# Grouped-query attention with a cached K and V, on one core: all eight heads of the first projection per chunk, and its loads reordered over two DMA queues

## Chip, cores, metric

One core of a Trainium2 chip. The metric is device time in microseconds (us) of one execution, which most executions of a kernel here repeat within 0.3%. The profile's span is some 1.8 us shorter than the time.

## The reference

Two independent problems A and B of the same shape, bfloat16, whose outputs are concatenated:

```python
B, Sq, D = 16, 32, 1024            # 512 tokens
Hq, Hkv, Sk, Dh = 32, 4, 512, 128
q = (x @ wq).reshape(B, Sq, Hq, Dh).transpose(0, 2, 1, 3)
k, v = repeat(k_cache, 8, axis=1), repeat(v_cache, 8, axis=1)
p = softmax(einsum("bhqd,bhkd->bhqk", q, k) * Dh ** -0.5)
o = einsum("bhqk,bhkd->bhqd", p, v)
return o.transpose(0, 2, 1, 3).reshape(B, Sq, Hq * Dh) @ wo
```

## The kernel before

TensorE runs one long fixed sequence: queries, scores, values and output projections are interleaved so that it never has to wait. Only the first twenty microseconds have nothing to interleave: there the queries of the first eight heads (A's first key/value group) are made while their data arrive. The contraction over D = 1024 has eight chunks of 128. Chunks 0 and 1 of x are transposed on TensorE, the others by transposing DMA loads, two chunks each. Each head needs one matmul per chunk, 128x128 weights against 512 tokens.

```python
NF = REP - 2            # 6 heads at first: 8 - 2
HC = DC // 2            # 4 chunks per weight tile
...
load_x(TT // 2, TT, nc.scalar)                 # ScalarE's queue
nc.scalar.preload_act_table_set("natural_log_exp_and_others")
load_x(0, TT // 2)                             # SyncE's queue, as all without nc.scalar
load_w0(0, 1, 0, NF // 2)                      # load_w0(chunk from, to, head from, to)
load_w0(0, 1, NF // 2, NF)
load_w0(1, 2, 0, NF, nc.scalar)
load_x_transposed(2)                           # chunks 2 and 3 of x
load_w0(2, 3, 0, NF, nc.scalar)
load_w0(3, 4, 0, NF)
load_w0(0, HC, NF, REP)                        # heads 6 and 7, chunks 0 to 3
load_w0(HC, HC + 1, 0, REP)
load_x_transposed(HC)
...
warm_up(22)                                    # matmuls on constants
... # transposes of chunks 0 and 1
for ts in ((0, TT // 2), (TT // 2, TT)):
    first_heads(range(0, NF // 2), (0,), *ts)  # six half-width matmuls
first_heads(range(NF // 2, NF), (0,))
first_heads(range(NF), (1, 2, 3))
first_q += [...]                               # two more PSUM banks come free
first_heads(range(NF, REP), range(HC))
first_heads(range(REP), range(HC, DC - 1))
```

All loads are given to two queues, and the framework that builds the program (below: the builder) gives each DMA a semaphore, a counter that tells of its landing and for which an instruction can wait.

## Time and profile before

| kernel before | |
|---|---|
| time, median of 6 runs | 343.27 us (342.94 to 343.48) |
| span of the profiled run | 340.8 us |
| TensorE busy | 99% of the span |
| first projection, L531 | 67 matmuls, with starts from 4.2 to 18.2 us |

In the profile PE is TensorE's matmuls, PEld its weight loads, SPq and ACTq the queues on which SyncE and ScalarE issue DMAs; a line "start, length, what" in the chain of work tells what the end of the program waited for at that time. "q_ps L531" is the first projection, L301 the later ones. The prediction below shows and reads the lines.

### The profile page before, as it was taken

Reading aid. Unit: us, or ns where it says so; the run is one execution under the profiler, and the core shown is the slowest. Engines: PE = TensorE matmul, PEld = TensorE weight load, DVE = VectorE, ACT = ScalarE, POOL = GpSimd, SP = SyncE. Lnnn points to the kernel's source line nnn. Section 1 sums busy time; section 2 is a strip of 40 time slices with the busy share of each in tenths; the row PEclk is TensorE's granted clock in tenths of the full one; section 3 lists DMA queues with packets and bytes.
Section 4 is the critical chain, followed back from the end, with each engine's and each line's share of the span. In section 5 each row is a group of like instructions: output and inputs, shape, how many; then the busy total and the mean of one; then the engine's idle time right before and its main releaser. Section 6 shows DMA issues by size and latency. Waiting matters only on the chain.

```text
span 340.8 us, 5475 instructions
## 1 busy us (share of the span) xinstructions
PE 336.7 (99%) x2113; PEld 213.0 (62%) x2113; DVE 265.2 (78%) x335; ACT 185.4 (54%) x208; POOL 46.7 (14%) x206
## 2 busy tenths in 40 slices
PE   8999999999999999999999999999999999999996
PEld 5456666666666666666666666666666666666555
DVE  0047988888888898888888898879888888889540
ACT  2067666666757667666645544554554555555110
POOL 0001111011111111110012221222122101111100
PEclk9999999999999999999999999999999999999999
DMA  8999999989996998899999966998449996430001
GB/s 208 297 186 270 287 248 223 188 238 259 312 266 159 241 230 227 214 291 296 317 297 285 239 125 148 344 283 211 125 106 300 355 193 161 105 100 13 17 19 33
DMA packets 128622, 71.70 MB, mean 210 GB/s; under 512 B 76880, under 2 KB 127824, under 8 KB 128592
## 3 DMA queue, kind: packets, MB, share of 16 engines
q1 hardware_dynamic: 127504, 69.68, 84.1%
q0 software_dynamic: 384, 1.05, 0.9%
q10 hardware_dynamic: 704, 0.59, 0.6%
q8 instruction: 17, 0.28, 0.4%
q14 instruction: 13, 0.11, 0.1%
HBM read 50.59 MB, written 2.10 MB: 155 GB/s over the span
## 4 chain that ended last, share of the span: by engine, by line
PE 99%; ACT 0%; issue 0%; ACTq 0%
PE f_ps L320 32%; PE q_ps L301 28%; PE s_ps L357 16%; PE ob L425 16%; PE q_ps L531 4%; PE q_ps L513 1%; PE xT_ps L521 0%; ACT o_sb L329 0%; ACTq L329 0%
## 5 line engine op out<-in xcount | busy, mean ns | idle before, releaser
L365 ACT ACTIVATE p_sb<-s_ps,shift 128x1024 bf16<-128x1024 f32 x128 | 142.7, 1115 | 97.5 <-PE s_ps L357 85.0
L376 DVE TRANSPOSE_TENSOR_REDUCE parts<-p_sb 128x32 f32<-128x1024 bf16 x128 | 158.8, 1240 | 20.9 <-ACT p_sb L365 19.3
L320 PE MATMUL f_ps<-wo_sb,oT 128*128 128x512 bf16 (+1 forms) x544 | 132.3, 366 | 0.0
L301 PE MATMUL q_ps<-xT,wq_sb 128*128 128x512 bf16 x448 | 116.9, 379 | 0.0
L357 PE MATMUL s_ps<-qT,kT 128*128 128x256 bf16 x512 | 76.8, 273 | 0.0
L425 PE MATMUL ob<-p_sb,v_sb 128*128 128x256 bf16 x512 | 76.8, 273 | 0.0
L320 PEld LDWEIGHTS <-oT 128*128 128x128 bf16 x544 | 53.2, 98 | 35.3
L357 PEld LDWEIGHTS <-kT 128*128 128x128 bf16 x512 | 56.9, 113 | 28.3
L301 PEld LDWEIGHTS <-wq_sb 128*128 128x128 bf16 x448 | 43.8, 98 | 32.2
L425 PEld LDWEIGHTS <-v_sb 128*128 128x128 bf16 x512 | 50.1, 98 | 20.0
L447 DVE TENSOR_TENSOR oT<-r,ob 128x512 bf16<-128x512 f32 x64 | 43.9, 686 | 19.9 <-PE ob L425 19.4
L411 DVE STREAM_TRANSPOSE r<-rall 128x512 f32<-128x512 f32 x64 | 44.2, 691 | 1.1
L309 ACT CAST qT<-q_ps 128x512 bf16<-128x512 f32 x56 | 32.7, 583 | 16.5 <-PE q_ps L301 16.5
L394 POOL COPY half<-cs 64x32 f32<-64x32 f32 x32 | 6.5, 204 | 231.4 <-DVE cs L384 231.3
L329 ACT CAST o_sb<-f_ps 128x512 bf16<-128x512 f32 (+1 forms) x17 | 9.5, 559 | 23.6 <-PE f_ps L320 23.6
L531 PE MATMUL q_ps<-xT,w_sb 128*128 128x512 bf16 (+1 forms) x67 | 14.4, 374 | 0.0
L384 DVE TENSOR_REDUCE cs<-parts 128x32 f32<-128x128 f32 x32 | 12.0, 376 | 1.1
L406 DVE RECIPROCAL rall<-sums 128x32 f32<-128x32 f32 x32 | 10.2, 320 | 3.3 <-POOL sums L403 3.3
L553 DVE CAST qT<-q_ps 128x512 bf16<-128x512 f32 x4 | 2.5, 684 | 12.8 <-PE q_ps L531 12.8
L531 PEld LDWEIGHTS <-w_sb 128*128 128x128 bf16 x67 | 6.5, 100 | 7.5 <-DMA w_sb<-in_A_wq_dram 0.3
L553 ACT CAST qT<-q_ps 128x512 bf16<-128x512 f32 x4 | 2.1, 599 | 12.3 <-PE q_ps L531 12.3
L331 POOL DMA_DIRECT2D out_dram<-o_sb x8 | 4.6, 574 | 29.3 <-ACT o_sb L329 29.3
(25 smaller groups left out, 48.2 us busy)
## 6 DMA issues: line engine op xcount, KB each, us to landing
v_sb<-in_A_v_cache_dram SPq DMA_DIRECT2D x16, 512.0 KB, 6.0
wq_sb<-in_B_wq_dram SPq DMA_DIRECT2D x8, 1024.0 KB, 5.8
wo_sb<-in_A_wo_dram SPq DMA_DIRECT2D x8, 1024.0 KB, 7.6
v_sb<-in_B_v_cache_dram SPq DMA_DIRECT2D x16, 512.0 KB, 4.8
wo_sb<-in_B_wo_dram SPq DMA_DIRECT2D x8, 1024.0 KB, 8.5
wq_sb<-in_A_wq_dram SPq DMA_DIRECT2D x5, 1024.0 KB, 6.7
wq_sb<-in_A_wq_dram SPq DMA_DIRECT2D x2, 512.0 KB, 7.3
kT<-in_A_k_cache_dram SPq DMA_TRANSPOSE x64, 4.4
```

Of the source, the lines that this page charges most:

```text
L301: nc.tensor.matmul(ps[:], lhsT=w[:, dc, (h % 4) * DH:(h % 4 + 1) * DH], rhs=xT[pr][:, dc, :], start=(dc == 0), stop=(dc == DC - 1),)
L309: nc.scalar.copy(out=qT[pr, g][:, :, hl, :], in_=ps[:].rearrange("p (b s) -> p b s", s=SQ),)
L320: nc.tensor.matmul(ps[:, 0:width], lhsT=oT[pr, tt][:, h, :], rhs=wo_tiles[pr, nh, h // REP][:, h % REP, off:off + width], start=(h == 0), ...
L357: nc.tensor.matmul(s_ps[:, c, :], lhsT=kT[:, i % GRP, c, :], rhs=qT[pr, g][:, b, :, :].rearrange("p h s -> p (h s)"), start=True, stop=True,)
L365: nc.scalar.activation(out=p_sb[:], in_=s_ps[:], func=ACTF.Exp, bias=shift[:], scale=SCALE)
L376: nc.vector.tensor_reduce(out=parts[k][:, q, :, :].rearrange("p c h -> p (c h)"), in_=st[i]["p"][:].rearrange("p c (h s) -> p (c h) s", s=SQ),
L384: nc.vector.tensor_reduce(out=cs[:], in_=parts.pop(k)[:].rearrange("p q c h -> p q h c"), axis=AX.X, op=ALU.add,)
L406: nc.vector.reciprocal(out=rall[:, k, :], in_=quad.pop(k)[:])
L411: nc.vector.transpose(out=r[:].rearrange("p n s -> p (n s)"), in_=rall[:, k, o * 2 * REP:(o + 1) * 2 * REP] .unsqueeze(2).to_broadcast([P, ...
L425: nc.tensor.matmul(ob[j][:, q, :], lhsT=v_sb[:, i % GRP, c, :], rhs=st[i]["p"][:, c, :], start=(c == 0), stop=(c == KC - 1),)
L447: nc.vector.tensor_tensor(out=out, in0=rcp.pop(j)[:].rearrange("p (q h) s -> p q h s", h=REP), in1=ob.pop(j)[:].rearrange("p q (h s) -> p ...
L531: nc.tensor.matmul(first_q[h][:, ts], lhsT=w0[dc // HC][:, dc % HC, h * DH:(h + 1) * DH], rhs=xT[0][:, dc, ts], start=(dc == 0 and t0 == 0 ...
```

## The change

The intent: since the two banks of PSUM (the memory that TensorE's results go to) for heads 6 and 7 are free after chunk 1, all eight heads can be done from chunk 2 on (and heads 6 and 7 catch up on chunks 0 and 1), and the loads can then come in the order of need, spread over both queues.

```diff
             load_w0(0, 1, 0, NF // 2)
-            load_w0(0, 1, NF // 2, NF)
-            load_w0(1, 2, 0, NF, nc.scalar)
+            load_w0(0, 1, NF // 2, NF, nc.scalar)
+            load_w0(1, 2, 0, NF)
+            load_w0(0, 2, NF, REP, nc.scalar)
+            load_w0(2, 3, 0, REP, nc.scalar)
             load_x_transposed(2)
-            load_w0(2, 3, 0, NF, nc.scalar)
-            load_w0(3, 4, 0, NF)
-            load_w0(0, HC, NF, REP)
+            load_w0(3, HC, 0, REP)
@@
-            first_heads(range(NF), (1, 2, 3))
+            first_heads(range(NF), (1,))
             first_q += [psum.tile([P, NW], FP32, name="q_ps", tag="ob")[:] for _ in range(2)]
-            first_heads(range(NF, REP), range(HC))
-            first_heads(range(REP), range(HC, DC - 1))
+            first_heads(range(NF, REP), (0, 1))
+            first_heads(range(REP), range(2, DC - 1))
```

## The prediction

> **What bounds the kernel now.** I read the page first (busy shares and slices), then the chain of work that ended last in order of time, then the busy time by stretches, then the timeline of TensorE over the first 20 us, and last the DMA issues of that stretch. The question is only whether TensorE ever stands still, because every matmul of this program stays where the change leaves it.
>
> The page and the busy time by stretches:
>
> ```profile
> span 340.8 us, 5475 instructions
> PE 336.7 (99%) x2113; PEld 213.0 (62%) x2113; DVE 265.2 (78%) x335; ACT 185.4 (54%) x208; POOL 46.7 (14%) x206
> ...
> PE   8999999999999999999999999999999999999996
> ```
>
> ```profile
> 18.50:120.00 101.50, 101.50 (x632) 63.80 (x631) 83.90 (x104) 68.56 (x83) 12.95 (x60) 1.00 1.07 242
> 120.00:240.00 120.00, 120.00 (x764) 77.03 (x762) 104.55 (x131) 70.97 (x77) 20.28 (x84) 1.00 0.97 252
> ```
>
> The columns of the second fence are the stretch, its length, then PE, PEld, DVE, ACT and POOL busy. On the page all slices but the first and the last are at 90% or more; in the stretches PE is busy for 101.50 of 101.50 us and 120.00 of 120.00 us. A loaded engine can hide short gaps under pipelined matmuls, so I check the pace as well, in the chain:
>
> ```profile
> 0.93 2.52 PE q_ps L513 x22
> 3.45 0.95 PE xT_ps L521 x8
> 4.40 0.84 PE q_ps L531 x6
> 5.24 0.01 issue
> 5.25 13.36 PE q_ps L531 x61
> 18.61 3.45 PE q_ps L301 x16
> ```
>
> In the steady stream 16 matmuls of 512 columns take 3.45 us, 0.2156 us each. The 61 of the first projection take 13.36 us, 0.2190 each, so their surplus is 13.36 - 61 x 0.2156 = 0.21 us. That, plus whatever the first 6 lost, is the whole stock that a better start can draw on. The chain never leaves TensorE before its last half microsecond.
>
> Where the surplus lies is in the timeline of the start, cut into narrow windows so that a first start can be read off each line:
>
> ```profile
> 4.20 0.76 PEld L531 LDWEIGHTS <-w_sb 128*128 128x128 bf16 x6
> 5.24 2.08 PEld L531 LDWEIGHTS <-w_sb 128*128 128x128 bf16 x11 [0.29 <-DMA w_sb<-in_A_wq_dram]
> ```
>
> ```profile
> 4.75 0.89 PE L531 MATMUL q_ps<-xT,w_sb 128*128 128x256 bf16 x4
> ```
>
> ```profile
> 6.99 0.62 PE L531 MATMUL q_ps<-xT,w_sb 128*128 128x512 bf16 x2
> ```
>
> The six half-width matmuls start at 4.20; the fourth of them at 4.75, so three took 0.55 us, 0.18 each. The other three run at 0.11 each and are issued by 4.75 + 3 x 0.11 = 5.08. The next starts at 5.24 to 5.25, held by the weights of heads 3 to 5: a wait of **0.17 us** (the 0.29 is the weight-load side of the same wait). The last line holds the final matmul of chunk 1 (start 6.99) and the first of chunk 2; the second ends at 7.61 with a duration of 0.38, so it starts at 7.23, 0.24 after its predecessor in place of 0.216: a wait of **0.03 us**, on the arrival of chunk 2's transposed x. From there to 18.61 the pace is 0.2158.
>
> **What the Trainium skill says.** "TensorE: Matmul & The Clock Gate", part 1 on the clock gate: the array runs at half speed until it has been active for some 3.4 us of a free-running window, 106.7 ns against 55.6 ns for 128 columns, 426.7 against 215.7 ns for 512. The trace agrees: 22 warm-up matmuls of 128 columns need 2.52 us (0.107 apart plus the last one's tail), the full-width ones are 0.216 apart, and the step lies at about 4.7 us, between the third and fourth half-width matmul. The slow half-width matmuls are thus a matter of the clock, not of loads, and the change cannot buy back their 0.2 us. "DMA: Bandwidth & Descriptors", section "Issuing engines are not separate DMA queues": DMAs issued by different engines run on the same 16 DMA engines, and using several saves only issue time. Its section "Queues, rings and completion order": each DMA engine alternates between the queues that have work, packet by packet. So what moves to ScalarE's queue is not carried faster; it shares the bandwidth with SyncE's and passes what waits behind on that queue. The case's trace shows an issue costing 0.43 to 0.58 us for a plain load and 1.33 us for the first transposing one. The last column of these two stretches is the rate in GB/s, 354 and then 165 where the transposing load (256-byte packets) runs:
>
> ```profile
> 3.00:4.00 1.00, 1.00 (x12) 0.75 (x10) 0.20 (x1) 0.00 (x0) 0.00 (x0) 1.00 1.07 354
> 5.00:6.00 1.00, 0.99 (x7) 0.40 (x5) 0.00 (x0) 0.00 (x0) 0.00 (x0) 1.00 1.21 165
> ```
>
> The issues and landings:
>
> ```profile
> 1.25 0.93 SPq L474 DMA_DIRECT2D w_sb<-in_A_wq_dram  x2
> 2.22 1.33 SPq L468 DMA_TRANSPOSE xT<-in_A_x_dram  x1
> ```
>
> ```profile
> w_sb<-in_A_wq_dram ACTq DMA_DIRECT2D x1, 192.0 KB, 3.7
> w_sb<-in_A_wq_dram SPq DMA_DIRECT2D x1, 96.0 KB, 3.5
> ```
>
> ```profile
> w_sb<-in_A_wq_dram ACTq DMA_DIRECT2D x1, 192.0 KB, 4.3
> xT<-in_A_x_dram SPq DMA_TRANSPOSE x1, 5.0
> ```
>
> Landing means issue plus the last column: chunk 1's weights 1.34 + 3.7 = 5.04; heads 3 to 5 of chunk 0 1.75 + 3.5 = 5.25 (exactly the held matmul); chunk 2's weights 1.83 + 4.3 = 6.13; chunk 2's x 2.22 + 5.0 = 7.22 (exactly the second hold).
>
> **The change part by part.** No matmul, copy or byte is added: 67 matmuls before and after, 2 MB of first weights before and after. Only orders move. Nine weight loads become nine: SyncE gives heads 3 to 5 of chunk 0 to ScalarE and takes chunk 1; ScalarE takes chunk 0-1 of heads 6 and 7 (128 KB) and chunk 2 of all eight (256 KB); SyncE's chunk 3 grows to eight heads and the load of the last two heads for four chunks goes.
>
> 1. Heads 3 to 5 of chunk 0 go out at 1.34 on ScalarE's queue in place of 1.75, with 224 KB on that queue up to its end. The like load on SyncE's queue, also 224 KB deep and issued at 1.25, lands at 1.25 + 2.9 = 4.15. So about 4.4; needed at 5.08. Saves the **0.17 us**.
>
> 2. Chunk 1 moves to SyncE at 1.75 and is 416 KB deep there. Before, 320 KB deep landed at 5.25 on SyncE, and on ScalarE 320 KB at 5.04 and 512 KB at 6.13, or 1.09 us for 192 KB while the queues share. 96 KB more is then about 0.55 us: landing near 5.8. It is needed at 5.08 + 3 x 0.216 = 5.72. Cost about **0.1 us**, between 0 and 0.4.
>
> 3. Heads 6 and 7 for chunks 0 and 1 now come before chunk 2: four matmuls, 4 x 0.216 = 0.86 us, which were taken from after chunk 3. They cost nothing in sum, and move the need of chunk 2 from 7.2 to 5.72 + 6 x 0.216 + 0.86 = 7.88. Their weights, 352 KB deep on ScalarE's queue, land near 5.3 and are needed at 7.0.
>
> 4. The transposed x of chunks 2 and 3 is still issued at 2.22, but behind 416 KB in place of 320 KB, with ScalarE's queue 608 in place of 512 KB deep: 192 KB more, at some 300 GB/s 0.65 us. Landing near 7.22 + 0.65 = 7.87 against 7.88. The margin is nil, so I put down half of the old wait and some: **0.05 us** on average, against 0.03 now. The weights of chunk 2, 96 KB deeper than before, land near 6.7: no wait.
>
> 5. SyncE's list is one load shorter, so everything after chunk 3 goes out about 0.5 us earlier. Nothing waited there: no gap from 7.23 to 18.61. Worth zero. The same holds for all later loads.
>
> Sum: -0.17 - 0.03 + 0.10 + 0.05 = **-0.05 us**; at best, with neither new wait, -0.20 us, 0.06% of the time. ScalarE's longer issuing (to about 2.8 us) is over before its first copy at 4.01.
>
> **The rivals.** First, *the full gain of 0.2 us*: chunk 1 comes in time after all. For it: data were already moving at 354 GB/s between 3 and 4 us, so the order and not the rate may decide. It would give 343.3. Second, *a new wait in place of the old one*: chunk 1 or the transposed x comes late by up to 0.4 us each. For it: both margins computed above are at zero or below. It would give 343.5 to 344.1. Third, *the clock*: a TensorE stall near 5 us could put off the full clock, or a different phase of the window shift the step by a microsecond or so; against it, the step lies before the stalls, and the three runs of before differ by only 0.54 us. Fourth, *the intent fulfilled in a way the profile doesn't show*: earlier first loads pulling the whole stream forward by microseconds. Against it, TensorE is at 0.216 us per matmul from 5.25 on; there are no microseconds to pull.
>
> **Range and chances.** The median before is 343.48, runs lie from 342.94 to 343.48. Less 0.05 and allowing for the centre of those runs lying a little under the median, I put 343.3. The scatter of single runs is larger than the effect, so the range is that scatter plus the worst new waits: 342.6 to 344.0. A change over 2% needs 6.9 us; the surplus to draw on is 0.2 us, and a loss of that size would need a stall some seventeen times as long as the longest one estimated (0.4). Chances: faster 0.004, same 0.99, slower 0.006.
>
> **What would show it.** Right: the weight-load wait of 0.29 us on the weights gone or moved; the 61 full-width matmuls in 13.2 to 13.5 us; the start of the steady stream between 18.3 and 18.7; from there to the end the same length. Step 1 is wrong if the first full-width matmul still waits at 5.2; step 2 if no hold appears near 5.7; step 4 if there is a hold of over 0.3 us near 7.9. The whole is wrong if TensorE shows a gap over 1 us before 20 us, or if the stretch after it changes its length.

## The result, and the profile after

| | before | after |
|---|---|---|
| time, median of 6 runs | 343.27 us | 344.29 us (343.45 to 344.54) |
| span of the profiled run | 340.8 us | 342.4 us |

The ratio of after to before is 1.0026, with a 95% interval of 1.0013 to 1.0039. A ratio is computed as the mean time of one kernel's fast runs over that of the other's fast runs of the same rounds, so it is not quite the ratio of the medians. The change costs 1.02 us between the medians, 0.9 us between the means; the prediction had -0.05 us and a range that ended at 344.0.

First, where the time is not. The weight loads of the later projections (L301) and of the output projections (L320), before and then after; the times are those of the first and the last start:

```profile
L301 PEld LDWEIGHTS <-wq_sb x448: 97/98/98, 18.2 to 168.4; 128*128 128x128 bf16 x150
L320 PEld LDWEIGHTS <-oT x544: 97/98/98, 169.2 to 337.3; 128*128 128x128 bf16 x182
```

```profile
L301 PEld LDWEIGHTS <-wq_sb x448: 97/98/98, 19.8 to 170.0; 128*128 128x128 bf16 x150
L320 PEld LDWEIGHTS <-oT x544: 97/98/98, 170.7 to 338.8; 128*128 128x128 bf16 x182
```

From the first to the last, 319.1 and 319.0 us pass: the whole stream after the start is the same and is only shifted. The loss lies before 20 us. The chain of work that ended last, after, in that stretch:

```profile
0.82 2.79 DMA x_sb<-in_A_x_dram
3.60 0.02 issue
3.63 5.95 DMA w_sb<-in_A_wq_dram
9.58 0.05 issue
9.62 0.39 PE q_ps L531
...
10.06 10.09 PE q_ps L531 x46
```

Before, this chain had nothing but TensorE. Now it starts with the landing of ScalarE's half of x at 3.60, goes on with a weight load issued at 3.63 that takes 5.95 us, and comes to TensorE only at 9.62. Two lines say which load that is and how long TensorE stood for it: the issue on ScalarE's queue, and the wait of TensorE:

```profile
3.63 0.33 ACTq L474 DMA_DIRECT2D w_sb<-in_A_wq_dram  x1
```

```profile
PE q_ps L531 <- DMA w_sb<-in_A_wq_dram: 0.9, 1, 0.9
```

It is ScalarE's fourth load, chunk 2's weights for all eight heads. Read as idle time the wait is 0.85 us; a matmul's duration here is 0.379 us but the next starts 0.216 us after it, so the delay of the start is 0.85 + 0.379 - 0.216 = 1.01 us.

Why does a load on ScalarE's queue wait for x? No line of the code asks for that. The compiled program's instruction list does. ScalarE's instructions after:

```text
2 L465 DMACopy x_sb<-in_A_x_dram 128x2x256
3 L480 LoadActFuncSet
4 L474 DMACopy w_sb<-in_A_wq_dram 128x384
5 L474 DMACopy w_sb<-in_A_wq_dram 128x2x256
6 L474 DMACopy w_sb<-in_A_wq_dram 128x1024 [waits DMAHW0_49]
```

The landings of all DMAs of both queues are told by eight semaphores, DMAHW0 to DMAHW7, used in turn; a ninth DMA takes the first one's and must wait until that has landed. Which load is the ninth follows the order in which the builder places the instructions of all engines in time, and it places ScalarE's function table load (row 3) ahead of rows 4 to 6, which puts row 6 behind SyncE's fifth load. Before, the ninth load was that of heads 6 and 7 on SyncE's queue:

```text
5 L474 DMACopy w_sb<-in_A_wq_dram 128x4x256 [waits DMAHW0_49]
```

It waited for nothing: SyncE came to it at 4.22 us, and x had landed at 3.74. The wait was in the program before, and no view of its profile shows a wait that is over when it is reached.

A second difference is the rate at which DMA engines move data. After, in the stretch from 5 to 6 us (last column GB/s; before had 165):

```profile
5.00:6.00 1.00, 1.00 (x5) 0.55 (x4) 0.00 (x0) 0.00 (x0) 0.00 (x0) 1.00 1.16 94
```

The second profile of after, below, has 171 there and the same delay of chunk 2, so this dip is not what the loss rests on.

And a third is no part of the change: the clock of TensorE. In the profile of before it came up to full speed at 4.7 us, in that of after at 6.2 us, as the distance of the matmuls' starts shows. The experiments show that this differs from run to run.

### The profile page after: what moved, and what is told of

Same layout as the page of the kernel before. It is cut to its first block, busy times and chain, and to the rows that moved or that the text cites. A ratio compares the mean times of both kernels' runs of the same rounds, so it can differ in the third digit from the quotient of the medians.

```text
span 342.4 us, 5436 instructions
## 1 busy us (share of the span) xinstructions
PE 335.4 (98%) x2074; PEld 213.4 (62%) x2113; DVE 265.4 (78%) x335; ACT 185.4 (54%) x208; POOL 47.0 (14%) x206
## 4 chain that ended last, share of the span: by engine, by line
PE 95%; DMA 3%; issue 1%; ACT 0%; ACTq 0%
PE f_ps L320 31%; PE q_ps L301 28%; PE ob L425 17%; PE s_ps L357 16%; PE q_ps L531 3%; DMA w_sb<-in_A_wq_dram 2%; DMA x_sb<-in_A_x_dram 1%; DMA out_dram<-o_sb 0%; ACT o_sb L329 0%; ACTq L698 0%; ACTq L329 0%; ACT p_sb L365 0%; ACTq L365 0%
## 5 line engine op out<-in xcount | busy, mean ns | idle before, releaser
L320 PE MATMUL f_ps<-wo_sb,oT 128*128 128x512 bf16 (+1 forms) x524 | 127.6, 366 | 0.6
L301 PE MATMUL q_ps<-xT,wq_sb 128*128 128x512 bf16 x430 | 113.0, 379 | 0.6
L320 PEld LDWEIGHTS <-oT 128*128 128x128 bf16 x544 | 53.2, 98 | 35.3
L301 PEld LDWEIGHTS <-wq_sb 128*128 128x128 bf16 x448 | 43.8, 98 | 32.2
L531 PE MATMUL q_ps<-xT,w_sb 128*128 128x512 bf16 (+1 forms) x66 | 15.2, 390 | 0.9 <-DMA w_sb<-in_A_wq_dram 0.9
```

The source lines that it names most:

```text
L301: nc.tensor.matmul(ps[:], lhsT=w[:, dc, (h % 4) * DH:(h % 4 + 1) * DH], rhs=xT[pr][:, dc, :], start=(dc == 0), stop=(dc == DC - 1),)
L320: nc.tensor.matmul(ps[:, 0:width], lhsT=oT[pr, tt][:, h, :], rhs=wo_tiles[pr, nh, h // REP][:, h % REP, off:off + width], start=(h == 0), ...
L531: nc.tensor.matmul(first_q[h][:, ts], lhsT=w0[dc // HC][:, dc % HC, h * DH:(h + 1) * DH], rhs=xT[0][:, dc, ts], start=(dc == 0 and t0 == 0 ...
```

## The experiments

Theory 1: chunk 2's weights come late because of the semaphore, and that is the loss. Rivals: the bytes and their order on the queues (theory 2, that a transposing load beside plain ones makes the DMA engines stall, is a form of it), the matmul order, the clock. All runs gave correct results.

**Before again.** The same kernel with a comment added.

> The kernel before, with a comment added, as a second look at its profile and as the measure of the noise. All theories: ratio 1.000 within 0.001, median 343.0 to 343.5. The theory that the phase of the TensorE clock sets the spread of before: the first full-speed matmul may come anywhere between 4.5 and 8 us in this second profile, and the start of the steady stream moves with it between 18.4 and 19.3 us.

Measured: ratio 0.9997 (0.9976 to 1.0017), median 343.42 us. The second profile has a span of 341.8 us and the steady stream from 19.2 us, 1.0 us later than the first. The stretch from 6 to 7 us in it:

```profile
6.00:7.00 1.00, 1.00 (x4) 0.37 (x3) 0.00 (x0) 0.00 (x0) 0.00 (x0) 1.00 1.17 240
```

PE is busy for the whole microsecond, as it is in the first profile, but with 4 full-width matmuls (in brackets) where the first profile has 7: they start 0.427 us apart up to 6.6 us, and 0.216 us apart from 6.9 us on. The column of the granted clock, third from the end, reads 1.00 in both, so this can only be seen in the pace. Not all of the 1.0 us is the clock: in this profile the weights of heads 0 to 2 landed at 4.47, so that the projection began at 4.52 and not at 4.20, while the old waits of 0.17 and 0.03 us are gone; some 0.9 us are left for the pace. It follows that the start of before alone moves by a microsecond from run to run, that the first profile was an early one (its execution took 342.66 us, less than any of the six timed runs), and that two single profiles can't be compared to better than that. The change's time should depend on it less, because chunk 2 waits for a load; no profile of the changed kernel with an early clock is there to show it.

**After again.**

> The changed kernel again, with a comment added: a second sample of its profile and its ratio on one chip with the three that follow. Theory 1 (the late issue of chunk 2's weights, from the reused semaphore, sets the start of chunk 2): ScalarE issues them again within 0.1 us of the landing of its own half of x, they land 8.8 to 9.8, and TensorE starts chunk 2 within 0.1 us of that. Ratio 1.002 to 1.004. If chunk 2 starts on something else in this profile, theory 1 holds only in part.

Measured: ratio 1.0039 (1.0012 to 1.0065), median 344.25 us. The chain:

```profile
3.85 5.81 DMA w_sb<-in_A_wq_dram
...
9.70 0.39 PE q_ps L531
```

x landed 0.2 us later than in the first profile of after (3.82), the weights were issued 0.2 us later, and TensorE started chunk 2 at 9.70 in place of 9.62, again 0.04 to 0.05 us after the landing. The delay of that start was 1.01 us once more.

**The table load behind ScalarE's loads.** One line moved, to make another load the ninth.

```diff
-            nc.scalar.preload_act_table_set("natural_log_exp_and_others")
...
             load_w0(2, 3, 0, REP, nc.scalar)
+            nc.scalar.preload_act_table_set("natural_log_exp_and_others")
```

> The changed kernel with one line moved: the load of ScalarE's function table comes after ScalarE's four weight and x loads, not after the first. The program then gives the reused semaphore (the ninth load waits for the landing of the first) to chunk 3's weights on SyncE's queue, not to chunk 2's on ScalarE's. Theory 1 (chunk 2's weights were issued 1.3 us late because they waited for the first load's landing, and then stood behind all that went out meanwhile): issue near 2.3 in place of 3.63, landing near 7 in place of 9.58, no hold of over 0.3 us at chunk 2, start of the steady stream 18.3 to 18.9 in place of 19.99, time 343.0 to 343.6, ratio to before 0.999 to 1.001. Rival (more bytes lie ahead of chunk 2's weights on ScalarE's queue, so they land late whenever they are issued): landing stays near 9, time near 344.3, ratio 1.003. Rival (the new matmul order costs by itself): ratio 1.003 as well.

Measured: ratio 1.0011 (0.9977 to 1.0046), runs from 342.23 to 346.17 us; so wide an interval decides nothing, the profile has to. The wait is gone from ScalarE's queue and chunk 2's weights go out at 2.31, but the last column of their row of issues says that they land 6.3 us later, at 8.6 and not near 7:

```profile
w_sb<-in_A_wq_dram ACTq DMA_DIRECT2D x1, 256.0 KB, 6.3
```

And the chain now holds TensorE one chunk earlier, at chunk 1's weights, which landed at 6.18 in the profile of after. First the chain, then the rates:

```profile
1.75 5.62 DMA w_sb<-in_A_wq_dram
...
7.41 2.55 PE q_ps L531 x11
```

```profile
6.00:7.00 1.00, 0.68 (x3) 0.09 (x1) 0.00 (x0) 0.00 (x0) 0.00 (x0) 1.00 0.31 34
```

34 GB/s, for a microsecond. Single packets of ScalarE's queue took up to 2.1 us there and ended together at 7.4 us. So the semaphore is what delays the issue, but to issue earlier is not simply to land earlier. Theory 1 alone is not enough: it had the weights land near 7 and no hold.

**The same once more**, to see whether this stall is chance.

> The version with the table load moved behind ScalarE's loads, a second sample. Its first profile showed chunk 2's weights issued at 2.31 as meant, but chunk 1's landing at 7.37 in place of 6.18, in a stretch in which packets stood still for up to 2.1 us. Theory 2 (with three loads at once, a transposing one on SyncE's queue beside plain ones on ScalarE's, the DMA engines stall for 0.7 to 2 us and whatever is then under way is late; which load that is differs from run to run): wide scatter again, 342.2 to 345, median between before and the changed kernel, 343.3 to 344.2, and in the profile a stretch of 1 us between 5 and 8 us under 120 GB/s. Theory 1 alone (only the semaphore): scatter as before, 0.6 us, median within 0.3 of before.

Measured: ratio 1.0011 (0.9996 to 1.0026), median 343.93 us, runs from 342.92 to 344.27, a scatter of 1.35 us and so less wide than expected. Same picture, with chunk 1's weights landing at 7.20:

```profile
1.75 5.45 DMA w_sb<-in_A_wq_dram
```

```profile
6.00:7.00 1.00, 0.00 (x0) 0.00 (x0) 0.00 (x0) 0.00 (x0) 0.00 (x0) 1.00 0.36 58
```

**The kernel before with a fourth load on ScalarE's queue**, x's half split in two.

```diff
-            load_x(TT // 2, TT, nc.scalar)
+            load_x(TT // 2, TT - 1, nc.scalar)
+            load_x(TT - 1, TT, nc.scalar)
```

> The kernel before, with ScalarE's half of x loaded by two DMAs of 64 KB in place of one of 128 KB. The matmul order, the bytes and their order on both queues stay; ScalarE now issues four loads, and its fourth, chunk 2's weights, becomes the ninth of the program and waits for the landing of the first. Theory 1: issue of chunk 2's weights after 3.2 us in place of 1.83, landing at 8 to 9.5 in place of 6.1, chunk 2 starts 1 to 2 us late, time 344.2 to 345.2, ratio 1.003 to 1.005. Rivals (bytes on the queue, matmul order, clock): nothing of theirs changes, ratio 0.999 to 1.001.

Measured: ratio 1.0027 (1.0006 to 1.0048), median 344.44 us. The wait is made as foreseen, and the load is late:

```profile
3.31 0.33 ACTq L474 DMA_DIRECT2D w_sb<-in_A_wq_dram  x1
```

Issued 0.02 us after the first load's landing at 3.29, landed at 8.43; chunk 2 starts at 8.48. But the split also made the second half of x land at 4.15, so the first projection began late, at 4.49, and in this profile the clock came up only near 7.3 us. That the fourth load waits and lands late is shown. That it makes the 0.9 us is not: with the late start and the late clock TensorE waited only 0.04 us for it here (8.48 in place of 8.44).

**The changed loads with the old matmul order.**

```diff
-            first_heads(range(NF), (1,))
+            first_heads(range(NF), (1, 2, 3))
...
-            first_heads(range(NF, REP), (0, 1))
-            first_heads(range(REP), range(2, DC - 1))
+            first_heads(range(NF, REP), range(HC))
+            first_heads(range(REP), range(HC, DC - 1))
```

> The changed kernel's loads with the old matmul order (six heads through four chunks, then the last two heads). Theory 1: the landing of chunk 2's weights near 9.6 sets the start of chunk 2, and 52 full-width matmuls still follow it in place of 48, so 4 x 0.216 = 0.86 us on top of the changed kernel: 345.0 to 345.4, ratio 1.005 to 1.006. Rival (the new matmul order is what costs): the loss goes away, ratio 1.000.

Measured: ratio 1.0061 (1.0035 to 1.0087), median 345.13 us; the new order is not what costs. Where chunk 2's weights are late it saves time, since four matmuls are done before the hold and not after it: the ratio is 1.0061 with the old order, 1.0026 and 1.0039 with the new. In the chain the same load holds TensorE:

```profile
3.57 5.55 DMA w_sb<-in_A_wq_dram
...
9.17 1.04 PE q_ps L531 x4
```

**The exchange of heads 3 to 5 and chunk 1 alone**, in the kernel before.

```diff
-            load_w0(0, 1, NF // 2, NF)
-            load_w0(1, 2, 0, NF, nc.scalar)
+            load_w0(0, 1, NF // 2, NF, nc.scalar)
+            load_w0(1, 2, 0, NF)
```

> The kernel before, with one pair of loads exchanged as in the change: heads 3 to 5 of chunk 0 go to ScalarE's queue, chunk 1 to SyncE's. Matmul order as before, three loads on ScalarE. This is steps 1 and 2 of the prediction alone: heads 3 to 5 land near 4.4 (0.17 us saved), chunk 1 near 5.8 to 6.2 (0 to 0.4 us lost, less where the clock of TensorE comes up late). Time 343.0 to 343.7, ratio 0.999 to 1.001. If the exchange were what costs in the change, ratio 1.002 to 1.003.

Measured: ratio 0.9998 (0.9984 to 1.0011), median 343.20 us. In its profile heads 3 to 5 landed at 4.38 and no longer held anything; chunk 1 landed at 6.02, and as the clock had come up before 4.1 us there, TensorE waited for it (start delayed by 0.71 us), and later, by 0.33 us, for chunk 3's. So the exchange trades one wait for another and is not the loss.

**Chunk 2's weights on SyncE's queue behind the transposing load**: as late as in the change, without the wait.

```diff
-            load_w0(2, 3, 0, REP, nc.scalar)
             load_x_transposed(2)
+            load_w0(2, 3, 0, REP)
```

> The changed kernel with chunk 2's weights on SyncE's queue behind the transposing load, so that they are issued near 3.75, as late as in the changed kernel (3.63 and 3.85), but by the length of the queue and with no semaphore wait, and with nothing large left on ScalarE's queue. If it is the late issue alone that costs, whatever causes it: landing 9.3 to 9.9, chunk 2 starts there, ratio 1.003. If the late issue costs through what is under way beside it (chunk 3's weights of 256 KB go out on the other queue at the same time in the changed kernel and share the bandwidth with chunk 2's): here chunk 2's have the engines to themselves and land 8.2 to 8.8, ratio 0.999 to 1.001.

Measured: ratio 1.0000 (0.9985 to 1.0016), median 343.20 us. The issue and the landing:

```profile
3.61 0.57 SPq L474 DMA_DIRECT2D w_sb<-in_A_wq_dram  x1
```

```profile
w_sb<-in_A_wq_dram SPq DMA_DIRECT2D x1, 256.0 KB, 4.3
```

Same bytes, issued at the same 3.6 us: landed at 7.95 in place of 9.58, and TensorE never waited for it. This is the run that corrects theory 1. The late issue alone does no harm. In the change, chunk 3's weights, also 256 KB, go out on SyncE's queue at 3.78 and are carried beside chunk 2's: they landed together there, at 9.58 and 9.80. The packets of the changed kernel's first profile agree. Chunk 2's, the only ones of 2 KB on ScalarE's queue, began at 6.6 us. From 6.5 us to the landing (packets, MB, share of the engines' time; q1 is SyncE's queue, q10 ScalarE's):

```profile
q1 hardware_dynamic: 908, 0.66, 94.7%
q10 hardware_dynamic: 144, 0.26, 32.9%
```

Chunk 2's 0.26 MB shared the engines with 0.66 MB of SyncE's, which is chunk 3 and more of what comes behind it.

**The transposing load behind chunk 3's weights**, with the table load moved.

```diff
-            load_x_transposed(2)
             load_w0(3, HC, 0, REP)
+            load_x_transposed(2)
```

> The version with the table load moved (chunk 2's weights on ScalarE's queue at 2.31), with the transposing load placed behind chunk 3's weights on SyncE's queue; it becomes the ninth load and is issued near 3.6. Theory 2 (a transposing load beside plain ones on the other queue is what makes the engines stall): chunk 1's weights land at 5.4 to 6.2 in place of 7.2 to 7.4, chunk 2's at 6.3 to 7.3 in place of 8.6, no stretch under 120 GB/s before 7 us; chunk 2 then waits for the transposed x, landing 8.3 to 9.2. Ratio 0.999 to 1.002. If the stall came from three plain loads of the start on two queues and not from the transposing one: chunk 1's weights land after 6.8 again.

Measured: ratio 1.0004 (0.9991 to 1.0017), median 343.49 us. Chunk 1's load, issued at 1.75:

```profile
w_sb<-in_A_wq_dram SPq DMA_DIRECT2D x1, 192.0 KB, 3.7
```

It landed at 5.47, against 7.2 to 7.4 in the two runs that differ only in which comes first, the transposing load or chunk 3's weights; and no microsecond from 3 to 7 us fell under 250 GB/s; from 7 to 8 us, with the transposing load under way, it was 168. In this comparison, of one profile with two, the stall before 7 us came only with the transposing load ahead. Chunk 2's weights were missed: they landed at 8.07, not by 7.3, side by side with chunk 3's at 7.85. Chunk 2 then waited until 8.98 for the transposed x, as expected.

**Chunk 2's weights on SyncE's queue ahead of the transposing load.**

```diff
-            load_w0(2, 3, 0, REP, nc.scalar)
+            load_w0(2, 3, 0, REP)
             load_x_transposed(2)
```

> The changed kernel with chunk 2's weights on SyncE's queue, ahead of the transposing load; ScalarE keeps three loads and no load of the first eight waits. Under theories 1 and 2 both evils go: chunk 2's weights are issued near 2.2 and land near 6.3, nearly all plain loads of the start are over when the transposing one moves its data, which lands at 7.4 to 8.2; chunk 2 starts at 7.9 to 8.6 and the steady stream 18.3 to 19.0 us. Time 342.7 to 343.4, ratio 0.998 to 1.000. Rival (the matmul order costs): ratio 1.003. Rival (the bytes cannot come sooner): chunk 2 held until 9, ratio 1.002 or more.

Measured: ratio 0.9982 (0.9968 to 0.9996), median 342.52 us. Chunk 2's weights landed at 6.64, the transposed x at 7.62, and only chunk 1 was waited for:

```profile
1.75 3.87 DMA w_sb<-in_A_wq_dram
...
5.67 2.55 PE q_ps L531 x11
...
8.27 10.09 PE q_ps L531 x46
```

**Once more.**

> The fastest version so far (chunk 2's weights ahead of the transposing load, both on SyncE's queue) once more, as a second ratio and profile: 0.9972 to 0.9992, chunk 2 starts with no hold over 0.2 us, start of the steady stream 17.9 to 18.9 us depending on when the clock comes up.

Measured: ratio 0.9993 (0.9981 to 1.0006), median 343.24 us. Here the chain has no load in it at all; the clock came up late, near 6.4 us, and all loads were in time:

```profile
4.44 4.68 PE q_ps L531 x20
...
9.17 10.09 PE q_ps L531 x46
```

Of the two ratios only the first is clear of 1. The version is faster than the changed kernel, and faster than before by 0.2 to 0.6 us (the differences of the means of the two sets of rounds), which is at the edge of what can be told.

**Only two loads on ScalarE's queue**, the rest on SyncE's in the order of need.

```diff
-            load_w0(0, 2, NF, REP, nc.scalar)
-            load_w0(2, 3, 0, REP, nc.scalar)
+            load_w0(0, 2, NF, REP)
+            load_w0(2, 3, 0, REP)
             load_x_transposed(2)
```

> The changed kernel with only two loads left on ScalarE's queue (its half of x, then heads 3 to 5 of chunk 0) and the rest on SyncE's in the order of need: heads 0 to 2 of chunk 0, chunk 1, heads 6 and 7 of chunks 0 and 1, chunk 2, then the transposing load as the eighth. If what makes loads late is sharing the bandwidth with a later-needed load on the other queue, chunk 1 lands at 4.9 to 5.4 in place of 5.6 to 6.4, heads 6 and 7 near 6, chunk 2 at 6.2 to 7.2, the transposed x at 7.6 to 8.4, and no hold exceeds 0.2 us; ratio 0.997 to 0.9995, at or below the version with three loads on ScalarE's queue (0.9982 and 0.9993). If issue time on SyncE counts instead (the transposing load goes out 0.46 us later), chunk 2 is held until 8.5 and the ratio is 1.000 or more.

Measured: ratio 1.0004 (0.9990 to 1.0017), median 343.18 us. The landings came as foreseen (chunk 1 at 5.37, heads 6 and 7 at 5.75, chunk 2 at 7.21, the transposed x at 8.22), but with eight issues in a row SyncE came late to the later loads: that of chunks 5 and 6 went out at 7.69 and landed at 13.71, and TensorE started on it 0.31 us late. The ratio hoped for, at most 0.9995, did not come. And the rate:

```profile
6.00:7.00 1.00, 1.00 (x7) 0.41 (x6) 0.00 (x0) 0.00 (x0) 0.00 (x0) 1.00 0.86 90
```

There is a stall at the transposing load here too, with nothing left on ScalarE's queue. So traffic on the other queue is not needed for one. The two deepest, with 34 and 58 GB/s for a microsecond, had 256 KB under way on it; that it deepens the stall is not shown. What the DMA engines wait for in it stays open.

## Why the prediction was wrong

The chance of 0.99 for "within 2%" was right, and so was the reading that only the start was at stake. The size and the sign were not: 344.29 us lies 0.29 us over the range.

- **Step 1**, heads 3 to 5 of chunk 0: right. Predicted landing 4.4, measured 4.32 and 4.46; TensorE no longer waits for them.
- **Step 2**, chunk 1 near 5.8: measured 6.18 and 5.81. In the profiles of after it cost nothing, but by luck: the late clock had put off the need to 6.45; where the clock was early (the exchange alone) it cost 0.71 us, more than the 0.4 allowed, and 0.33 us with chunk 2's weights ahead of the transposing load.
- **Step 3**, the matmul order: right in kind, it put off the need of chunk 2 and cost nothing in sum; the old order with the new loads is slower still. The weights of heads 6 and 7 landed at 6.49 and 6.13, not near 5.3, but still in time.
- **Step 4** is the step that failed, in its last sentence: "The weights of chunk 2, 96 KB deeper than before, land near 6.7: no wait." They landed at 9.58 and 9.66. Two things went wrong in it. The issue was taken to follow the others ("ScalarE's longer issuing (to about 2.8 us)"), but it waited for the semaphore of the first load until 3.63 and 3.85. And issue to landing took 5.95 us, with SyncE's next loads beside it; on SyncE's queue ahead of them it took 4.3 us, and with that issue at 3.61 the ratio is 1.0000. So the late issue alone does not cost. Issued in time on ScalarE's queue, the weights landed at 8.6, and the hold moved to chunk 1: ratio 1.0011, twice, clear neither of 1 nor of the change's 1.0026. Late issue and neighbours together go with the 1.01 us delay of chunk 2 in both profiles, which is the size of the loss (between the medians 1.02 us, in the second set of rounds 0.80). That the whole of the loss is this delay is not shown to better than some 0.4 us: against the second profile of before, whose clock was late as well, the steady stream starts 0.6 us later (19.8 against 19.2); against the two profiles with the new matmul order, a late clock and no hold (chunk 2's weights on SyncE's queue behind the transposing load, and the second with them ahead of it) it is 0.9 to 1.0 us (18.8 and 18.9).
- The landing of **the transposed x**, also step 4: predicted 7.87, measured 7.58 and 7.11; it was not late.
- **Step 5**, nothing after chunk 3: right, the stream from there on has the same length.
- **The estimate of 300 GB/s** under all of these was too smooth. Beside the transposing load the rate fell to 94 GB/s for a microsecond in one profile of after (171 in the other), and to 34 in a variant.
- **The third rival**, the clock, was dismissed with "the three runs of before differ by only 0.54 us". It does move the start, by some 0.9 us between the two profiles of before; it does not explain the difference, since the ratio of six runs each is clear of 1 and was found again on another set of rounds (1.0039), while before against itself gave 0.9997.

## What to carry to other kernels

Count the loads in flight, over all queues: a program that tells landings by a fixed set of semaphores makes the next load wait for the oldest, and which load that is can change by moving an instruction that has nothing to do with it. Look for such waits in the compiled instruction list, since a wait that is over when it is reached shows in no profile and becomes one when the order changes. And read a load's time to landing together with what is issued on the other queue just after it: here the same 256 KB took 5.95 us with large, less urgent loads beside them and 4.3 us ahead of these on one queue.

## What the Trainium skill lacked or had wrong

- No page says what follows when the program's builder tells all landings by a fixed number of semaphores. Here there are eight, and the ninth load was issued 0.02 us after the landing of the first in all four profiles that have the wait on ScalarE's queue (3.605 to 3.626, 3.824 to 3.845, 3.550 to 3.571, 3.286 to 3.306 us).
- "DMA: Bandwidth & Descriptors", section "Issuing engines are not separate DMA queues", says that the DMAs interleave and that using several issuing engines saves only issue time. What interleaving can cost a load that is needed first it leaves out: 256 KB issued at 3.6 us landed after 5.95 us with the next load on the other queue, after 4.3 us with it behind on the same queue.
- The same page, section "Rules for kernel authors", says "A transpose next to ordinary DMAs needs nothing", in a row on wrong results. For the results that held in all runs. What it lacks is the time: beside the first transposing load the rate fell to 94, 90, 58 and 34 GB/s for a microsecond in four profiles (171 in the second of after), and in two of them chunk 1's weights landed at 7.2 to 7.4 us in place of 5.47.
- "TensorE: Matmul & The Clock Gate", part 1 on the clock gate, puts the step to full speed at around 4 us of activity, give or take 0.5, and also calls the window free-running. Here the first matmul is at 0.93 us in every profile and the step came between 3.8 and 7.3 us, 2.8 to 6.3 us later, a far wider scatter, which made some 0.9 us of difference between two profiles of the same kernel.
